# Moving the first query and key load and a 360-element load in a fused one-core kernel, and two small copies from ScalarE to GpSimd

## The chip, the cores and the metric

The kernel runs on one core of a Trainium2 chip. The metric is the time of one execution in microseconds of device time. Before the change it is 308.97 us, the median of three runs (307.27 to 309.54).

## What is computed

Three layers run one after the other on an input of 2 batches, 768 positions and 8 heads of 40 elements, in single precision. The first is a recurrent attention layer with exponential gates:

```python
m_new = np.maximum(f_gate[:, :, t] + m, i_gate[:, :, t])
f_stab = np.exp(f_gate[:, :, t] + m - m_new)
i_stab = np.exp(i_gate[:, :, t] - m_new)
C = f_stab * C + i_stab * outer(v_t, k_t)
n = f_stab * n + i_stab * k_t
y[:, :, t] = sigmoid(o_gate_t) * (C @ q_t) / max(|n . q_t|, 1)
```

The second multiplies half of `relu(x @ w_in)` by a normalised and position-mixed other half, and by `w_out`. The third mixes each position with the one before it and applies `w_k`, `w_v` and `w_r`.

## The kernel before, in words

**Blocks.** The recurrence is computed in chunks of 128 positions. There are 12 blocks (2 batches x 6 chunks), taken in the order of the list `SEQ`: chunk 0 of both batches, then chunk 1 of both, and so on. This text calls them block 0, block 1, block 2 and block 3 by their place in that order. Per block TensorE makes scores `sc` from queries and keys `qk` (line 463), a logarithmic decay `ld` (lines 471 to 475, or 495 from block 4 on), the inside part `av` (line 599), the state update `sp` from weighted keys `kw` (line 533), the part that comes from the state `cn` (`ip`, line 570), and at the end a transpose `tp` of the finished rows `x` (line 646). ScalarE takes the exponential of `ld` into `dt` (line 479), VectorE multiplies `dt` by `sc` (line 489). The transposed rows go into `xg` (a rounded part from ScalarE, line 660, and a rest from VectorE, line 235), and feed the products `up` and `vp` with `w_in`, which begin at about 35 us and keep TensorE filled from there on. All the later layers are matmuls of line 671.

**Who sets the order.** A planner in Python keeps an estimated clock for TensorE, VectorE, ScalarE and GpSimd and writes their instructions in the order that this clock gives; each engine then runs its list strictly in that order, and waits on semaphores for the others. Where the planner expects TensorE to be idle in the first blocks it writes dummy matmuls (`heat`, line 363, output `wp`). They are a fixed number of instructions, run whether or not TensorE would have had to wait.

**Loads.** Nearly all transfers are issued by the SyncE queue (SP), in the order of the code. Each takes one of eight semaphores in turn, so that a transfer is not issued before the one eight places ahead of it has landed. The first ones are the gates `fg` and `ig`, the identity `id_sb`, four output gates `og` (160 KB each), the queries and keys of block 0 in two halves of 160 KB (each 40 rows of 4 KB), then `kvq` of block 0, a third of `w_in`, the queries and keys of block 1, and so on. `bm_raw`, three columns of the block mask in 120 rows, is 360 separate elements of 4 bytes.

**The mask and the output gates.** ScalarE first takes the sigmoid of the four `og` tiles as they land (line 355), then copies the identity to `mask[:, 1]` (line 859), and only then begins with the exponentials. TensorE's third matmul of each first `ld` (line 475) reads that mask.

**The state.** For chunk 0 ScalarE copies `bm_raw` to `bm_sb` (line 546) and writes `cn` from `sp` with it (line 548). For later chunks `cn` is first multiplied by `dec` (line 543). `dec`, and the gate rows of all later chunks, come from a chain over all chunks at once, called G1 in the code: `f<-f,m`, `i<-i,m`, `f<-f,m`, a scan, and so on (lines 407 to 416) on VectorE, with two casts (`Lxc`, `Axc`) on ScalarE. Its end is `i<-i,f` (line 416), which TensorE transposes into `gpsc` (line 423). Two small transfers per row pair (`lt`, `rl`) then bring its results to where line 495 reads them.

**The repeated columns of x.** Each finished block `x` has 320 columns, and its columns 256 to 320 are copied to 320 to 384 (lines 627 and 628) before the transpose. For blocks 0 and 1 ScalarE makes this copy, for all others GpSimd.

**The weights.** The three thirds of `w_u` are split into two parts by a chain: two ScalarE operations (`wsq`, `wbits`, lines 274 and 278), two of VectorE (lines 284 and 288), a cast on ScalarE (line 297) and a subtraction on GpSimd (line 235).

Of the kernel before, what the change touches and what calls it, by code (L numbers as in the profile page):

```python
# [7 lines left out]
F32 = mybir.dt.float32  # L8
# [10 lines left out]
def tile_mlstm_gmlp_channelmix(  # L19
# [25 lines left out]
    SEQ = [6 * b + c for c in range(6) for b in range(2)]  # L45
    P = 128
    H, D = 8, 40
    DA = D + 1
# [3 lines left out]
    DM = H * D  # L52
# [6 lines left out]
    vec, act, pool, pe = nc.vector, nc.scalar, nc.gpsimd, nc.tensor  # L59
    sync = nc.sync  # L60
# [4 lines left out]
    at = tc.alloc_tile_pool(name="at", bufs=1, side="right")  # L65
# [59 lines left out]
    def use(e, cost, t=None):  # L125
        free[e] = max(free[e], clock[0] if t is None else t) + cost
        return free[e]
# [45 lines left out]
    def chain(key, *steps, ready=None):  # L173
        running.append(Chain(key, steps, clock[0] + 0.2 if ready is None else ready, 0.0))

    def finish(*keys, stall=True):
        for k in keys:
            while any(b[0] == k or b[0][0] == k for b in back):
                if not force_feed():
                    break  # L180
            for c in [c for c in running if c.has(k)]:
                while c in running and c.has(k):
                    advance(c.start(), skip=c)
                    if not c.open():
                        finish(split[0], stall=False)
                    if c in running and c.has(k):
                        issue(c)
        if stall:
            at_least(max([done.get(k, 0.0) for k in keys], default=0.0))
# [25 lines left out]
    def load(out, in_, kb, after=0.0):  # L215
        sync.dma_start(out=out, in_=in_)  # L216
        dma_free[0] = max(dma_free[0], after, clock[0] - 1.0) + max(0.5, kb / (360.0 if clock[0] > 20.0 else 230.0))
        return dma_free[0] + 1.8

    def page(name, dt=F32R, n=PG, keys=()):  # L220
        own("pg", 12, *keys)
        return base.tile([P, n if dt == I64 else PG], dt, tag="pg", name=name, bufs=12)[:, :n]
# [80 lines left out]
    def rows3(t, w):  # L303
        return t[:, :3 * w].rearrange("p (a b) -> p a b", a=3)
# [6 lines left out]
    fg = gp.tile([16, S], F32, name="fg")  # L311
    ig = gp.tile([16, S], F32, name="ig")
# [17 lines left out]
    def load_qk(i):  # L330
        b, c = divmod(i, NCH)
        t = at.tile([P, 2, 4, P], F32, tag="qk", name=f"qk{i}", bufs=2)
        for hh in range(2):
            e = load(t[64 * hh:64 * hh + D], qk[b, c, hh], 164)
        st["q", i], st["k", i] = t[:, 0], t[:, 1]
        st["at", i] = e

    def load_kv(i):
        b, c = divmod(i, NCH)
        n = H * D + H * DA + (3 * P if c > 0 else 0)  # L340
        t = at.tile([P, H * D + H * DA + 3 * P], F32, tag="kvq", name=f"kvq{i}", bufs=2)
        note(("kv", i), load(t[:, :n], kvq[b, c, :, :n], n * 0.5))
        st["kt", i] = t[:, :H * D].rearrange("p (h d) -> p h d", h=H)
        st["vt", i] = t[:, H * D:H * (D + DA)].rearrange("p (h d) -> p h d", h=H)
        if c > 0:
            st["qc", i] = t[:120, H * (D + DA):].rearrange("p (g t) -> p g t", g=3)

    def load_o(c):
        for b in range(B):
            o = st["o", b, c] = at.tile([P, DM], F32, tag="og", name=f"og{c}_{b}", bufs=9)  # L350
            st["ot"] = load(o, o_tok[b, c // 3, :, c % 3], 164)
# [15 lines left out]
    vec.memset(unit.bitcast(F32), 0.0)  # L367
    for t in first_.values():
        vec.memset(t.bitcast(F32), 0.0)
    for a in 'f i d o0 o1 q'.split():  # L370
        dict(f=lambda: sync.dma_start(out=fg, in_=f_gate), i=lambda: sync.dma_start(out=ig, in_=i_gate),
             d=lambda: sync.dma_start(out=id_sb, in_=ident), o=lambda: load_o(int(a[1])), q=lambda: load_qk(SEQ[0]))[a[0]]()

    pool.memset(ones, 1.0)
# [227 lines left out]
    def normalise(i):  # L602
        b, c = divmod(i, NCH)
        av, spare = st.pop(("av", i)), st.pop(("spare", i))
        osl = st["o", b, c].rearrange("p (h d) -> p h d", h=H)
        nn = st.pop(("nn", i)) if c > 0 else at.tile([P, H, DA], F32, tag="nn", name=f"nn{i}", bufs=2)
        dn = at.tile([P, H], F32, tag="dn", name=f"dn{i}", bufs=2)
        x = at.tile([P, 3 * P], F32, tag="x", name=f"x{i}", bufs=2)

        finish(*[("nn", i)] * (c > 0), stall=False)  # L610

        def clip():
            vec.tensor_scalar(out=spare, in0=nn[:, :, D], scalar1=1.0, scalar2=None, op0=ALU.max)
            pool.tensor_tensor(out=osl, in0=osl, in1=nn[:, :, :D], op=ALU.mult)
            return use("P", 0.82, free["V"])

        chain(("x", i),
              ("V", 0.41, lambda: vec.tensor_tensor(out=nn, in0=nn, in1=av, op=ALU.add)) if c > 0 else
              ("A", 0.4, lambda: act.copy(nn, av)),
              ("V", 0.08, clip),  # L620
              ("V", 0.15, lambda: vec.scalar_tensor_tensor(out=dn, in0=nn[:, :, D], in1=spare,
                                                           scalar=-1.0, op0=ALU.mult, op1=ALU.max), ("av", i)),
              ("V", 0.18, lambda: vec.reciprocal(out=dn, in_=dn)),
              ("V", 0.4, lambda: vec.tensor_tensor(out=x[:, :DM].rearrange("p (h d) -> p h d", h=H), in0=osl,
                                                   op=ALU.mult,
                                                   in1=dn.unsqueeze(2).to_broadcast([P, H, D]))),
              ("P", 0.2, lambda: pool.tensor_copy(x[:, DM:], x[:, 2 * P:DM])) if SEQ.index(i) >= 2 else
              ("A", 0.2, lambda: act.copy(x[:, DM:], x[:, 2 * P:DM])))
        st["x", i] = x

    xg = {}
# [139 lines left out]
    def w_in_load(nm, j, *qs):  # L771
        W.setdefault((nm, "raw"), [])
        for q in qs:
            raw = page(f"w_in{nm}{q}", I64, PG // 2, [f"w_{nm}{x}" for x in range(3)])[:, :512]
            W[nm, "raw"].append((q, raw, load(raw, w_in[j, q], 512)))
# [84 lines left out]
    free["A"] = 8.5  # L860
    free["P"] = 3.0
    hu = [rows3(page(f"w_u{q}"), 512) for q in range(2)]
    bm_raw = at.tile([120, 3], F32, name="bm_raw")
    m2 = gp.tile([96, 2, P], F32, name="m2")
    lpk = gp.tile([96, 6 * NCH], F32, name="lpk")
    clock[0] = 5.5
# [4 lines left out]
        for w in range(2):  # L871
            st["late"] = load(m2[:, w], mg[:, w:w + S], 48, 14.0)

    for a in 'k0 v0 q6 k6 v1 b v2 n'.split():
        dict(k=lambda: load_kv(SEQ[a != "k0"]), q=lambda: load_qk(SEQ[1]), n=lambda: load_qk(SEQ[2]),
             v=lambda: w_in_load("u", 0, int(a[1])), b=lambda: load(bm_raw, blockmask[:, 0:3 * DA:DA], 2))[a[0]]()
    w_in_split("u", hu)
# [42 lines left out]
    def position(p):  # L920
# [45 lines left out]
        def n1():  # L966
            intra(i, 1)
            normalise(i)
            if nn is not None:
                load_kv(nn)  # L970
            if p == 0:
                w_in_load("v", 1, 0)
                sync.dma_start(out=mu_sb, in_=mu)
            if p == 1:
                w_in_load("v", 1, 1)
                load_o(2)
                load_o(3)
            if p == 2:
                w_in_load("v", 1, 2)
                load_o(4)  # L980
            if p == 3:
                load_o(5)
            if n is not None:
                key_weights(n)
# [225 lines left out]
    for g in range(2 * B):  # L1210
# [17 lines left out]
        for j in range(3):  # L1228
            sl = slice(j * P, (j + 1) * P)
            prs = []  # L1230
            for f in range(8):
                k0, k1 = k2t[g, f][:, 0, sl], k2t[g, f][:, 1, sl]
# [126 lines left out]
```

## Time and profile before

| | us |
|---|---|
| median of three runs | 308.97 |
| the profiled execution, its own time | 308.54 |
| its span, first to last instruction | 305.5 |
| TensorE busy in the span | 294.4 |
| VectorE busy | 218.5 |
| ScalarE busy | 172.4 |
| GpSimd busy | 140.3 |

The profile shows one execution. A timeline row has the start, the duration (for a group of neighbours the length from the first's start to the last's end), the engine, the line, the operation, output and input, and the count; in square brackets stands how long the engine was idle just before, and what ended that. Single-precision matmuls are recorded as two passes each. Names stand without their numbers, so that `qk` is any block's; the place in time tells which.

### The profile page before, as it was taken

To read this page: it belongs to the slowest core of one execution; us is meant where nothing else is said; L and a number is where in the kernel's file an instruction comes from. 1 tells how busy PE (TensorE), PEld (TensorE's weight loads), DVE (VectorE), ACT (ScalarE), POOL (GpSimd) and SP (SyncE) were. 2 spreads that over 40 slices of the span, in tenths; PEclk is the share of its full clock that TensorE was granted. 3 is DMA by queue.
4 is the path that set the end of the run, shared out by engine and by line. 5 is a ranking of instruction groups with operands and counts; after the bars stand their busy time and mean duration, and the time that the engine had idled before them with its cause. 6 is when DMAs were issued, how large, how long until landed. Compare 5 with 4: busy or idle time off the path is not lost.

```text
span 305.5 us, 6000 instructions
## 1 busy us (share of the span) xinstructions
PE 294.4 (96%) x2233; PEld 273.3 (89%) x2233; DVE 218.5 (72%) x440; ACT 172.4 (56%) x383; POOL 140.3 (46%) x167
## 2 busy tenths in 40 slices
PE   8998898999889999999999999999999999999995
PEld 6776787787778887999999999999999999999995
DVE  7768696856697787746879989898856755745611
ACT  3764587676865555653254654686936845734610
POOL 5143324526679774733556637484426305303500
PEclk9999999999999999999999999999999999999999
DMA  6959665333223411554115212221010010000001
GB/s 154 291 165 288 195 226 171 137 116 114 56 69 98 138 46 50 174 157 165 43 45 172 81 41 86 89 86 44 3 43 21 2 43 24 0 35 32 1 21 43
DMA packets 13939, 28.77 MB, mean 94 GB/s; under 512 B 2407, under 2 KB 7783, under 8 KB 13911
## 3 DMA queue, kind: packets, MB, share of 16 engines
q1 hardware_dynamic: 13879, 28.33, 29.4%
q8 instruction: 17, 0.28, 0.4%
q0 software_dynamic: 32, 0.07, 0.2%
q14 instruction: 11, 0.09, 0.1%
HBM read 26.20 MB, written 1.97 MB: 92 GB/s over the span
## 4 chain that ended last, share of the span: by engine, by line
PE 71%; DVE 9%; ACT 6%; POOL 5%; DMA 4%; issue 2%; SPq 1%; POOLq 0%; DVEq 0%; ACTq 0%
PE spp L671 16%; PE kp L671 15%; PE vv L671 14%; PE wop L671 7%; PE up L671 5%; PE rp L671 5%; DMA bm_raw<-in_blockmask_dram 3%; PE vp L671 2%; DMA qk<-in_qk_dram 2%; POOL vn L235 2%; PE sc L463 1%; DVE sb L728 1%; DVE dt L508 1%; PE av L599 1%; SPq L216 1%
## 5 line engine op out<-in xcount | busy, mean ns | idle before, releaser
L1202 POOL TENSOR_TENSOR sq<-sq 128x384 f32<-128x384 f32 x32 | 29.9, 941 | 47.9 <-ACT sq L1201 47.8
L671 PE MATMUL spp<-wsp,vn 128*128 128x384 f32 x288 | 50.4, 334 | 0.0
L671 PEld LDWEIGHTS spp<-wsp,vn 128*128 128x128 f32 x288 | 49.9, 188 | 0.0
L671 PE MATMUL kp<-xk,wk 128*128 128x384 f32 x256 | 45.3, 334 | 0.0
L671 PEld LDWEIGHTS kp<-xk,wk 128*128 128x128 f32 x256 | 44.4, 188 | 0.0
L671 PE MATMUL vv<-wv,k 128*128 128x320 f32 x288 | 42.9, 309 | 0.0
L671 PEld LDWEIGHTS vv<-wv,k 128*128 128x128 f32 x288 | 42.4, 188 | 0.0
L235 DVE TENSOR_TENSOR k<-sq,k 128x384 fp32r<-128x384 f32 x32 | 26.2, 820 | 13.6 <-ACT k L1203 13.6
L671 PE MATMUL up<-xg,w_u 128*128 128x256 f32 x192 | 31.0, 295 | 0.0
L671 PE MATMUL vp<-w_v,xg 128*128 128x512 f32 x96 | 29.0, 417 | 1.9 <-ACT vr L740 0.9
L1099 POOL TENSOR_TENSOR vs<-vs,u 128x384 f32<-128x384 f32 x16 | 19.8, 1237 | 22.5 <-DVE vs L1098 21.1
L671 PEld LDWEIGHTS up<-xg,w_u 128*128 128x128 f32 x192 | 25.8, 190 | 1.0 <-DVE xg L235 0.2
L1201 ACT ACTIVATE sq<-kp 128x384 f32<-128x384 f32 x32 | 15.6, 490 | 16.8 <-PE kp L671 14.8
L284 DVE SCALAR_TENSOR_TENSOR wbits<-wsq,wbits 128x320 int32<-128x320 int32 (+1 forms) x27 | 20.9, 774 | 4.4 <-ACT wsq L274 3.5
L671 PE MATMUL wop<-gt,wo 128*128 128x384 f32 x128 | 22.8, 334 | 0.0
L671 PEld LDWEIGHTS wop<-gt,wo 128*128 128x128 f32 x128 | 22.2, 188 | 0.0
L671 PEld LDWEIGHTS vp<-w_v,xg 128*128 128x128 f32 x96 | 17.0, 189 | 5.7 <-ACT vr L740 1.4
L1242 DVE TENSOR_TENSOR ob<-rs,vv 128x320 f32<-128x320 f32 x12 | 5.8, 487 | 20.4 <-PE vv L671 19.3
L235 POOL TENSOR_TENSOR vn<-vr,vn 128x512 fp32r<-128x512 f32 x12 | 15.4, 1287 | 6.8 <-ACT vn L750 6.8
L1100 ACT CAST gt<-vs 128x384 fp32r<-128x384 f32 x16 | 8.2, 512 | 18.0 <-POOL vs L1099 18.0
L288 DVE SCALAR_TENSOR_TENSOR wsq<-wraw,wbits 128x320 int32<-128x320 int32 (+1 forms) x21 | 17.2, 821 | 0.3
L1141 DVE SCALAR_TENSOR_TENSOR tm<-x,mu_sb,tm 128x384 f32<-128x384 f32 x24 | 17.1, 748 | 0.0
(184 smaller groups left out, 571.4 us busy)
## 6 DMA issues: line engine op xcount, KB each, us to landing
kvq<-in_kvq_dram SPq DMA_DIRECT2D x10, 516.0 KB
qk<-in_qk_dram SPq DMA_DIRECT2D x24, 160.0 KB
wraw<-in_w_k_dram SPq DMA_DIRECT2D x6, 512.0 KB
wraw<-in_w_v_dram SPq DMA_DIRECT2D x8, 320.0 KB
wraw<-in_w_sp_dram SPq DMA_DIRECT2D x12, 192.0 KB
og<-in_o_tok_dram SPq DMA_DIRECT2D x12, 160.0 KB
out_dram<-ob SPq DMA_DIRECT2D x12, 160.0 KB
w_inu<-in_w_in_dram SPq DMA_DIRECT2D x3, 512.0 KB
```

What stands on the lines that cost most here:

```text
L216: sync.dma_start(out=out, in_=in_)
L235: eng.tensor_tensor(out=out, in0=a, in1=b.bitcast(F32), op=ALU.subtract)
L284: vec.scalar_tensor_tensor(out=t["bits"], in0=t["sq"].bitcast(I32), scalar=3, in1=t["bits"], op0=ALU.logical_shift_left, op1=ALU.bitwise_or)
L288: vec.scalar_tensor_tensor(out=t["sq"].bitcast(I32), in0=t["high"], scalar=SIGN, in1=t["bits"], op0=ALU.bitwise_and, op1=ALU.bitwise_or)
L463: pe.matmul(st["sc", i, x][:, h * P:(h + 1) * P], k_[64 * x:64 * x + D, h, :], q_[64 * x:64 * x + D, h, :], start=True, stop=True)
L671: pe.matmul(out[0], l, x, start=j == 0, stop=j == len(prs) - 1)
L1099: ("P", 1.29, lambda: pool.tensor_tensor(out=vs, in0=vs, in1=ut[b][:, d, sl], op=ALU.mult)),
L1100: ("A", 0.51, lambda: act.copy(gt[:, 0], vs)), ("V", 0.7, lambda: sub(vec, gt[:, 1], vs, gt[:, 0])))
L1141: return lambda: vec.scalar_tensor_tensor(out=t[:, c], in0=x[:, c, 1:], scalar=mu_sb[:, w, c:c + 1], in1=t[:, c], op0=ALU.mult, op1=ALU.add)
L1201: chain(("k2", g, f), ("A", 0.49, lambda: act.activation(out=sq, in_=ps, func=AF.Relu), ("kp", g, f)), ("P", 0.96, lambda: pool.tensor_ten ...
L1202: ("P", 0.96, lambda: pool.tensor_tensor(out=sq, in0=sq, in1=sq, op=ALU.mult)),
L1242: vec.tensor_tensor(out=ob, in0=rs, in1=ps, op=ALU.mult)
```

## The change

The list of the first loads, a letter per load, becomes `f i d q b o0 o1` where it was `f i d o0 o1 q`: the queries and keys of block 0 (`q`) go ahead of the four output gates (`o0`, `o1`), and `bm_raw` (`b`) is loaded there too, behind the identity and the queries. It is taken out of the later list, where it stood between the second and the third part of `w_in`. The copy of the repeated columns is made by GpSimd for blocks 0 and 1 too.

```diff
-    for a in 'f i d o0 o1 q'.split():
-        dict(f=lambda: sync.dma_start(out=fg, in_=f_gate), i=lambda: sync.dma_start(out=ig, in_=i_gate),
+    bm_raw = at.tile([120, 3], F32, name="bm_raw")
+    for a in 'f i d q b o0 o1'.split():
+        dict(b=lambda: load(bm_raw, blockmask[:, 0:3 * DA:DA], 2), f=lambda: sync.dma_start(out=fg, in_=f_gate), i=lambda: sync.dma_start(out=ig, in_=i_gate),
              d=lambda: sync.dma_start(out=id_sb, in_=ident), o=lambda: load_o(int(a[1])), q=lambda: load_qk(SEQ[0]))[a[0]]()
...
-              ("P", 0.2, lambda: pool.tensor_copy(x[:, DM:], x[:, 2 * P:DM])) if SEQ.index(i) >= 2 else
-              ("A", 0.2, lambda: act.copy(x[:, DM:], x[:, 2 * P:DM])))
+              ("P", 0.2, lambda: pool.tensor_copy(x[:, DM:], x[:, 2 * P:DM])))
...
-    bm_raw = at.tile([120, 3], F32, name="bm_raw")
...
-    for a in 'k0 v0 q6 k6 v1 b v2 n'.split():
+    for a in 'k0 v0 q6 k6 v1 v2 n'.split():
```

On the SP queue, the first loads before the change; a name in brackets is the semaphore that the instruction waits for:

```order
L372 DMA id_sb<-in_ident_dram 128x128
L216 DMA og_0_103<-in_o_tok_dram 128x320
L216 DMA og_1_105<-in_o_tok_dram 128x320
L216 DMA og_0_107<-in_o_tok_dram 128x320
L216 DMA og_1_109<-in_o_tok_dram 128x320
L216 DMA qk_111<-in_qk_dram 40x1024
L216 DMA qk_111<-in_qk_dram 40x1024 [waits DMAHW0_49]
L216 DMA kvq_153<-in_kvq_dram 128x648 [waits DMAHW1_49]
```

The same stretch after the change:

```order
L373 DMA id_sb<-in_ident_dram 128x128
L216 DMA qk_104<-in_qk_dram 40x1024 x2
L216 DMA bm_raw<-in_blockmask_dram 120x3x1
L216 DMA og_0_108<-in_o_tok_dram 128x320
L216 DMA og_1_110<-in_o_tok_dram 128x320
L216 DMA og_0_112<-in_o_tok_dram 128x320 [waits DMAHW0_49]
L216 DMA og_1_114<-in_o_tok_dram 128x320 [waits DMAHW1_49]
L216 DMA kvq_154<-in_kvq_dram 128x648 [waits DMAHW2_49]
```

The two halves of `qk` and `bm_raw` now stand ahead of all four `og`.

On ScalarE, from the first copy of `x` to the second (between about 20 and 33 us in the profile), before the change. The names are those of the paragraphs above; `w_u` is the cast of line 297:

```order
L628 COPY x_347<-x_347 128x64
L297 CAST w_u_148<-wsq 128x512
L660 CAST xg_412<-tp_413 128x3x128
...
L414 CAST Axc<-i_77 96x128
L628 COPY x_489<-x_489 128x64
L297 CAST w_u_148<-wsq 128x512
L479 ACTIVATE dt_0_539<-ld_0_532 128x512
L426 ACTIVATE egc<-gpsc 128x192
L910 ACTIVATE dec<-dps 120x36
L543 ACTIVATE cn_323<-cn_323,dec 120x123 x2
```

After the change, where line numbers differ by one or so:

```order
L660 CAST xg_407<-tp_408 128x3x128
L297 CAST w_u_150<-wsq 128x512
...
L415 CAST Axc<-i_77 96x128
L480 ACTIVATE dt_0_538<-ld_0_531 128x512
L427 ACTIVATE egc<-gpsc 128x192
L909 ACTIVATE dec<-dps 120x36
L297 CAST w_u_150<-wsq 128x512
L544 ACTIVATE cn_323<-cn_323,dec 120x123 x2
```

The two copies are gone, the first `xg` cast stands ahead of the first `w_u` cast, and the exponential `dt_0_538` of block 3 and `dec` stand ahead of the third `w_u` cast.

On VectorE one operation of the third part of `w_u`, `wbits<-wsq,wbits`, goes from ahead of the G1 chain to behind the second block's `x`. Before:

```order
L288 SCALAR_TENSOR_TENSOR wsq<-w_inu_162,wbits 128x512
L284 SCALAR_TENSOR_TENSOR wbits<-wsq,wbits 128x512
L407 TENSOR_TENSOR f_76<-f_76,m_151 96x128
L408 TENSOR_TENSOR i_77<-i_77,m_151 96x128
...
L624 TENSOR_TENSOR x_489<-og_1_105,dn_488 128x320
L288 SCALAR_TENSOR_TENSOR wsq<-w_inu_165,wbits 128x512
```

After:

```order
L288 SCALAR_TENSOR_TENSOR wsq<-w_inu_163,wbits 128x512
L408 TENSOR_TENSOR f_76<-f_76,m_152 96x128
L409 TENSOR_TENSOR i_77<-i_77,m_152 96x128
...
L625 TENSOR_TENSOR x_488<-og_1_110,dn_487 128x320
L284 SCALAR_TENSOR_TENSOR wbits<-wsq,wbits 128x512
L288 SCALAR_TENSOR_TENSOR wsq<-w_inu_165,wbits 128x512
```

The G1 chain now follows `wsq` of the second part directly. On TensorE the only difference of order is that the first transpose `tp` stands two dummy matmuls earlier; the number of matmuls is the same.

## Rows read from the trace of the kernel before

**Rows 1.** The page: span, busy time of each engine, granted TensorE clock in 40 slices.
```profile
span 305.5 us, 6000 instructions
PE 294.4 (96%) x2233; PEld 273.3 (89%) x2233; DVE 218.5 (72%) x440; ACT 172.4 (56%) x383; POOL 140.3 (46%) x167
PEclk9999999999999999999999999999999999999999
```
**Rows 2.** The chain that ended last, first 50 us: start, length, what.
```profile
4.08 4.69 DMA qk<-in_qk_dram
...
8.79 8.23 DMA bm_raw<-in_blockmask_dram
```
**Rows 3.** Timeline of TensorE, 0 to 40 us.
```profile
8.52 0.39 PE L475 MATMUL ld<-mask 128*128 128x512 bf16 x1
...
14.15 0.48 PE L463 MATMUL sc<-qk 40*128 40x128 f32 x2
14.91 1.13 PE L463 MATMUL sc<-qk 40*128 40x128 f32 x14 [0.28 <-DMA qk<-in_qk_dram]
...
18.80 2.02 PE L363 MATMUL wp<-id_sb 128*128 128x256 bf16 x12
...
27.38 0.48 PE L471 MATMUL ld<-unit,Axb 128*128 128x512 f32 x1 [0.59 <-DVE dt L489]
...
29.50 0.30 PE L423 MATMUL gpsc<-id_sb,i 96*128 96x96 f32 x1 [0.71 <-DVE i L416]
...
32.27 0.80 PE L533 MATMUL sp<-kvq,kw 128*120 128x123 f32 x6 [1.22 <-ACT dt L479]
...
39.06 0.50 PE L495 MATMUL ld<-rl,lt 128*128 128x512 f32 x1
```
**Rows 4.** Timeline of the SP queue, 0 to 26 us (issue times and lengths).
```profile
4.08 0.74 SPq L216 DMA_DIRECT2D qk<-in_qk_dram  x2
...
8.79 0.36 SPq L216 DMA_DIRECT2D bm_raw<-in_blockmask_dram  x1
10.01 0.33 SPq L216 DMA_DIRECT2D w_inu<-in_w_in_dram  x1
```
**Rows 5.** Timeline of ScalarE, 4 to 18 us.
```profile
7.81 0.47 ACT L355 ACTIVATE og<-og 128x320 f32<-128x320 f32 x1 [1.59 <-DMA og<-in_o_tok_dram]
8.19 0.28 ACT L859 CAST mask<-id_sb 128x128 bf16<-128x128 f32 x1
...
17.04 0.19 ACT L546 COPY bm_sb<-bm_raw 120x3 f32<-120x3 f32 x1 [1.84 <-DMA bm_raw<-in_blockmask_dram]
```
**Rows 6.** Timeline of ScalarE, 20 to 32 us.
```profile
20.52 0.62 ACT L297 CAST w_u<-wsq 128x512 fp32r<-128x512 f32 x1
21.19 0.48 ACT L660 CAST xg<-tp 128x384 fp32r<-128x384 f32 x1
...
24.16 0.59 ACT L479 ACTIVATE dt<-ld 128x512 f32<-128x512 f32 x1
...
30.41 0.24 ACT L628 COPY x<-x 128x64 f32<-128x64 f32 x1 [2.46 <-DVE x L624]
31.01 0.62 ACT L297 CAST w_u<-wsq 128x512 fp32r<-128x512 f32 x1 [0.36 <-DVE wsq L288]
31.54 0.59 ACT L479 ACTIVATE dt<-ld 128x512 f32<-128x512 f32 x1
```
**Rows 7.** Timeline of VectorE, 23 to 30 us.
```profile
24.39 1.36 DVE L407 TENSOR_TENSOR f<-f,m 96x128 f32<-96x128 f32 x1
...
26.64 0.69 DVE L489 TENSOR_TENSOR dt<-dt,sc 128x512 f32<-128x512 f32 x1
```
**Rows 8.** Timeline of GpSimd: the copy as it makes it for block 2.
```profile
39.12 0.29 POOL L627 COPY x<-x 128x64 f32<-128x64 f32 x1 [1.07 <-DVE x L624]
```
**Rows 9.** Stretches: busy PE, PEld, DVE, ACT, POOL; granted clock, DMA share, GB/s.
```profile
8.40:10.00 1.60, 1.60 (x13) 1.20 (x11) 1.44 (x6) 1.57 (x3) 0.00 (x0) 1.00 1.03 274
34.00:34.50 0.50, 0.50 (x6) 0.50 (x5) 0.24 (x2) 0.00 (x0) 0.00 (x0) 1.00 0.08 25
```

## The prediction

> **What bounds the kernel now.** I read the page first: TensorE is busy for 294.4 us of a span of 305.5 [rows 1]. From about 35 us on it is filled by matmuls whose number the change leaves alone. What can be won or lost is therefore TensorE's waiting in the first 35 us, and whatever moves TensorE there moves the end by the same amount, unless something later takes it back. The chain of waits, read next, goes through the landing of the first `qk` (4.08 to 8.77 us) and of `bm_raw` (8.79 to 17.02 us) [rows 2], the two transfers that the change brings forward. But the chain says only what ended last; whether TensorE stood still for it is in its own timeline. There five places tell [rows 3]:
> - `ld<-mask` at 8.52. The mask was cast on ScalarE from 8.19 to 8.47, behind the sigmoid of the fourth `og`, which began at 7.81, when that tile landed, after 1.59 us of idle time [rows 5]. So TensorE is already tied to the fourth `og`: landing, plus 0.71 us, is the start of this matmul.
> - The scores of block 1: two matmuls at 14.15, the other 14 at 14.91, ended by a `qk` landing. The 14 last 1.13 us, some 0.08 apart, so the third could have begun at about 14.3; it lost 0.6 us, more than the 0.28 of modelled idle time.
> - 0.59 us at 27.38 until VectorE's `dt`, 0.71 us at 29.50 until `i<-i,f`, the end of the G1 chain, and 1.22 us at 32.27 until ScalarE's `dt` of block 3.
>
> Neither the wait for `bm_raw` (1.84 us, ScalarE, at 17.04 [rows 5]) nor one for the first `qk` stands on TensorE: at 18.80 it has 12 dummy matmuls ahead of the transpose that the chain leads to [rows 3].
>
> **The loads: a loss.** The first `qk` moves ahead of four `og`, and is needed later than they are, since the scores stand behind `ld<-mask`. When does the fourth `og` land now? Lower bound: it moves only by what is issued ahead of it, 0.74 us for two `qk` and 0.36 for `bm_raw` [rows 4], with the gaps some 1.15 us, so at 8.95. Upper bound: transfers land in the order of issue, and the same bytes now end with the `og`. `bm_raw`'s issue at 8.79 and the next one's at 10.01 each waited for one half of the first `qk` (they stand eight places behind), so the whole set had landed by 10.0 [rows 4]. With 0.4 us for 360 small packets in front (an estimate: as much as `bm_raw`'s own issue; no row separates their cost, and nothing would be the lower end) that is 10.4. I take 9.8, 2.0 us later, nearer to the upper end, because the two halves landed 1.22 us apart: 160 KB in that time is 134 GB/s while all transfers together moved 274 GB/s [rows 9], so `qk` is held by some of the engines only, and an `og`, which needs them too, waits behind it.
>
> The Trainium skill, page DMA: Bandwidth & Descriptors, section on why a DMA increments its semaphore by 16, says that a transfer is spread over the largest number of engines up to 16 that divides its rows: 10 engines for 40 rows, 16 for 128. The half rate agrees with it. By that rule alone the `og` would land with the old end of `qk`, at 10.0, and the sum below would be 0.2 us higher.
>
> So `ld<-mask` starts 2.0 us late (1.15 to 2.6), at about 10.5. Queued behind it on TensorE are the rest of both `ld`, four dummy matmuls and the scores, and on ScalarE the table load and the exponentials; all move with it. The wait at the scores of block 1 gives back its 0.6 us, since TensorE now comes after that `qk` has landed. **Late by 2.0 - 0.6 = 1.4 us** (0.55 to 2.0) from there on; call it s.
>
> `bm_raw` early takes away ScalarE's 1.84 us of idle time, and what stood behind (`cn`, `nn`) then waits for TensorE's `sp` instead, which is s late. Gain on TensorE: none, since the transpose stands behind dummy matmuls, two fewer than before. If these did not cover it, it could gain up to 0.4 us, the 1.84 less `sp`'s own 1.4.
>
> **The copies: a gain.** GpSimd's copy costs 0.29 us [rows 8] where ScalarE's cost 0.24 [rows 6]. The first is covered by ten dummy matmuls (12 take 2.02 us [rows 3]). The second waits for `x`, which is there at 30.41 [rows 6] plus the 0.36 us found below, and is done at 31.1, before TensorE starts the `sp` that stands ahead of the second transpose. Without that cover the price is 0.05 us each. What counts is the order that it leaves behind on ScalarE and VectorE.
>
> First, the G1 chain. The transpose ends s - 0.3 late (two dummy matmuls of 2.02/12 us go behind it). ScalarE casts `xg` (0.48) at 20.9 + s and only then begins with `w_u`, at 21.36 + s where it was 20.52. From that cast to `dt` of block 2 (24.16) are 3.64 us of cast, GpSimd subtraction, two operations and a second cast, which keep their order; so `dt` runs from 25.0 + s to 25.6 + s. VectorE waits for it: it no longer has `wbits` ahead of the chain, and even if `f<-f,m` again takes 1.36 us [rows 7], it reaches its own `dt` before that. So VectorE's `dt` starts at 25.6 + s where it was 26.64 [rows 7], a change of s - 1.04 us, and `i<-i,f`, six operations on, follows it. With s = 1.4 TensorE's `gpsc` comes at 29.86 instead of 29.50. The 0.59 us are gone (`ld` of block 3 has its predecessor in time), and most of the 0.71: **gain 1.04 us**.
>
> Second, the 1.22 us. TensorE's `sp` of block 2 needs the bank that ScalarE's `dt` of block 3 (31.54) leaves. Before it ScalarE stood for 2.46 us, waiting for VectorE's `x` to copy its columns, then 0.36 us for the `w_u` cast [rows 6]. Both are now off its path: that `dt` follows the `Axc` cast directly, as soon as `ld` is there. TensorE starts that `ld` at 28.2 (27.38 - 0.59 + 1.4) and arrives at `sp` at 31.4 (32.27 + 0.36 - 1.22), 3.2 us later, while the `dt` itself takes 0.59. **Gain 1.22 us.** Late next is the third `w_u` cast, behind a VectorE operation more (some 0.7 us, as `dt` [rows 7]) and 0.36 us: at about 32 instead of 31.01. Its GpSimd half is needed only by the eighth `up` matmul, behind two `av`, a transpose and an `ld`.
>
> **The sum**, against the profiled execution's own 308.54 us (0.43 below the median of the runs): 308.54 + 2.0 - 0.6 - 1.04 - 1.22 = **307.7 us**. With the two bounds of the landing it is 306.8 and 308.3.
>
> **The rivals.**
> - *The `og` land hardly later than they are issued* (8.95), since engines serve several transfers at once: 308.54 + 1.15 - 0.6 - 2.26 = 306.8, and 306.4 if the `bm_raw` term's 0.4 came on top. Against it stands the order of landings.
> - *Slower: the rows of block 4 become the wait.* The last `rl` transfer is queued behind loads that wait for TensorE's `av` of block 1, so it lands s late, while TensorE would reach `ld<-rl,lt` at 38.2 instead of 39.06 [rows 3]. If they land past 39.06 the gains are lost and s stays: 308.54 + 1.4 = 309.9. It decides only if they landed within 1.4 us of use before; against it, transfers had all but stopped by 34.0 to 34.5 (25 GB/s [rows 9]).
> - *The change does not do what it says:* ScalarE's own row of work further on takes the gain back, and the loss with it: 308.5.
> - *The clock falls.* The granted clock is 1.00 (2.4 GHz) throughout [rows 1], also beside the wait of 1.22 us; a wait of 2.0 has no row. At 1.2 GHz the 5.6 us from the mask at 8.52 to the scores at 14.15 [rows 3] would double at most: 308.54 + 1.4 + 5.6 - 2.26 = 313.3. The Trainium skill, page TensorE: Matmul & The Clock Gate, Part 1, says that an idle stretch can halve the clock; no run here shows it for so short a one.
>
> **How the numbers follow.** Forecast 0.47, early landing 0.22, nothing 0.14, late rows 0.12, clock 0.05. A measurement of this kernel can tell about 1% (3.1 us) from no change. Only early landing, with its term and a low run, reaches past that downward (0.08), only the clock and a part of the late rows upward (0.06): same 0.86. The range runs from early landing with its 0.4, less some of the runs' own spread (305.9), to the late rows (309.9).
>
> **What would show it.** In the changed profile the fourth sigmoid should start near 9.8, `ld<-mask` near 10.5 after a wait of about 2 us, the scores of block 1 without a wait near 16.3, no wait of over 0.3 us at `sp` of block 2 near 31.4, and line 495 near 38.2. If the sigmoid starts before 9 the early landing holds; if 495 waits, the late rows. A wait at the first transpose for GpSimd's copy would make the cover wrong.

## The result and the profile after

The changed kernel takes 305.39 us (median of nine executions), the kernel before 308.46 beside it; the ratio is 0.9892, 95% interval 0.986 to 0.9924, so 1.1% faster. Three of the nine (311.0 to 312.5 us, mean granted clock 0.975 to 0.978) are left out of the ratio, as such slow executions are from the ratios below; the other six take 304.9 to 305.7 with spans of 303.1 to 303.7. The profiled execution took 305.08 us with a span of 303.1, 2.4 below the span of [rows 1]. The forecast was 307.7, the range 305.9 to 309.9: the median lies below it, and those three executions lie above it.

The page of the changed kernel, as in [rows 1]:
```profile
span 303.1 us, 5998 instructions
PE 293.2 (97%) x2233; PEld 272.7 (90%) x2233; DVE 218.3 (72%) x440; ACT 171.9 (57%) x381; POOL 141.1 (47%) x169
PEclk9999999999999999999999999999999999999999
```
TensorE runs the same 2233 matmuls, so what went is its waiting. The page shows only half of that as idle time (9.9 us against 11.1) and the other half as busy time (293.2 against 294.4): a busy matmul can hold a wait, as the scores of block 1 did in [rows 3], 0.28 us idle for 0.6 lost. The timeline is the better witness. TensorE's timeline, at the places of [rows 3] (start, length, line, what, and in brackets the idle time before it and what ended it):
```profile
9.48 0.39 PE L476 MATMUL ld<-mask 128*128 128x512 bf16 x1 [1.29 <-ACT mask L859]
...
15.11 1.16 PE L464 MATMUL sc<-qk 40*128 40x128 f32 x16
...
20.57 0.49 PE L646 MATMUL tp<-id_sb,x 128*128 128x128 f32 x3
...
26.95 0.48 PE L472 MATMUL ld<-unit,Axb 128*128 128x512 f32 x1
...
28.50 0.30 PE L424 MATMUL gpsc<-id_sb,i 96*128 96x96 f32 x1
...
29.89 0.73 PE L534 MATMUL sp<-kvq,kw 128*120 128x123 f32 x6
...
36.61 0.50 PE L496 MATMUL ld<-rl,lt 128*128 128x512 f32 x1
```
Read against [rows 3], the first matmul with the mask is 0.96 us late (9.48 against 8.52), the scores of block 1 run without a wait, `gpsc` is 1.00 early, `sp` of block 2 is 2.38 early and line 496 (495 before) is 2.45 early. No wait is left at 26.95, 28.50 and 29.89. The end keeps those 2.4 us.

ScalarE in the changed kernel, as in [rows 5] and [rows 6]:
```profile
8.35 0.88 ACT L355 ACTIVATE og<-og 128x320 f32<-128x320 f32 x2 [0.20 <-DMA og<-in_o_tok_dram]
9.14 0.28 ACT L859 CAST mask<-id_sb 128x128 bf16<-128x128 f32 x1
...
16.08 0.19 ACT L547 COPY bm_sb<-bm_raw 120x3 f32<-120x3 f32 x1
17.15 0.82 ACT L549 ACTIVATE cn<-sp,bm_sb 40x123 f32<-40x123 f32 x3 [0.88 <-PE sp L534]
...
28.09 0.60 ACT L480 ACTIVATE dt<-ld 128x512 f32<-128x512 f32 x1 [1.05 <-PE ld L476]
...
30.74 0.62 ACT L297 CAST w_u<-wsq 128x512 fp32r<-128x512 f32 x1 [1.37 <-DVE wsq L288]
```
The fourth sigmoid, second of the pair at 8.35, begins near 8.8 where it began at 7.81. `bm_sb` no longer waits, but `cn` behind it waits 0.88 us for TensorE. The `dt` of block 3 now stands ahead of the `w_u` cast and waits only for its own `ld`. VectorE and GpSimd, as in [rows 7] and [rows 8]:
```profile
25.75 0.69 DVE L490 TENSOR_TENSOR dt<-dt,sc 128x512 f32<-128x512 f32 x1 [0.71 <-ACT dt L480]
...
27.82 0.63 DVE L417 TENSOR_SCALAR i<-i,f 96x128 f32<-96x128 f32 x1
```
```profile
19.77 0.63 POOL L628 COPY x<-x 128x64 f32<-128x64 f32 x1 [0.59 <-DVE x L625]
...
29.44 0.63 POOL L628 COPY x<-x 128x64 f32<-128x64 f32 x1 [1.07 <-DVE x L625]
```
VectorE's `dt` is 0.89 us earlier and the end of the G1 chain, `i<-i,f`, 1.00. GpSimd's copies take 0.63 us each, twice the 0.29 of [rows 8].

### The profile page after: what moved, and what is told of

Read it like the earlier page. It is cut to its first block, busy times and chain, and to the rows that moved or that the text cites. A ratio compares the mean times of both kernels' runs of the same rounds, so it can differ in the third digit from the quotient of the medians.

```text
span 303.1 us, 5998 instructions
## 1 busy us (share of the span) xinstructions
PE 293.2 (97%) x2233; PEld 272.7 (90%) x2233; DVE 218.3 (72%) x440; ACT 171.9 (57%) x381; POOL 141.1 (47%) x169
## 4 chain that ended last, share of the span: by engine, by line
PE 76%; DVE 8%; ACT 6%; POOL 5%; issue 2%; DMA 1%; SPq 1%; POOLq 0%; DVEq 0%; ACTq 0%
PE spp L671 16%; PE kp L671 15%; PE vv L671 14%; PE wop L671 7%; PE up L671 5%; PE rp L671 5%; PE vp L671 2%; PE sc L464 2%; PE av L600 2%; POOL vn L235 2%; PE sp L534 1%; DMA og<-in_o_tok_dram 1%; DVE sb L728 1%; DVE dt L509 1%; SPq L216 1%
```

## The experiments

**The kernel before, again.** No edit.

> The kernel before, once more as a kernel of its own, to see the span of every run beside its time (so far only one run of it shows both: 308.54 us with a span of 305.5, 3.04 us around the span, while the changed kernel's runs have 1.7 to 2.0 us around it). Theory A (the change moves TensorE in the first 32 us and nothing else): the spans lie at 305.5 within 0.3 us and the times at 307.5 within 0.3 us. Rival B (the kernel before has a start that varies from run to run, since one of its early waits does): the spans themselves spread over 1 us or more, as its times do (307.03 to 309.54).

Measured: median 308.38 us, ratio 0.9987 (0.9957 to 1.0018), with spans of 305.4 to 308.0: rival B holds. Its profile is not that of [rows 1]: the span is 308.0 and the granted clock falls in the fifth of 40 slices. The PEclk row of the page, TensorE's timeline, and four stretches (busy PE, PEld, DVE, ACT, POOL; granted clock, DMA share, GB/s):
```profile
PEclk9999599999999999999999999999999999999999
```
```profile
26.97 0.48 PE L471 MATMUL ld<-unit,Axb 128*128 128x512 f32 x1 [0.61 <-DVE dt L489]
...
29.09 0.30 PE L423 MATMUL gpsc<-id_sb,i 96*128 96x96 f32 x1 [0.71 <-DVE i L416]
...
31.86 1.42 PE L533 MATMUL sp<-kvq,kw 128*120 128x123 f32 x6 [1.22 <-ACT dt L479]
...
41.48 0.49 PE L495 MATMUL ld<-rl,lt 128*128 128x512 f32 x1
```
```profile
29.00:32.00 3.00, 1.69 (x12) 1.35 (x13) 1.72 (x7) 1.64 (x5) 0.70 (x1) 0.87 0.89 306
32.00:35.00 3.00, 3.00 (x26) 2.42 (x27) 1.79 (x6) 0.97 (x4) 1.25 (x2) 0.50 0.35 109
35.00:38.00 3.00, 3.00 (x18) 2.47 (x18) 0.72 (x2) 0.89 (x2) 0.00 (x0) 0.50 0.12 45
38.00:41.00 3.00, 3.00 (x41) 2.82 (x39) 2.15 (x7) 0.94 (x4) 0.81 (x1) 0.99 0.39 88
```
The three waits are those of [rows 3], to 0.02 us. But in the last of them the granted clock falls from 1.00 (2.4 GHz) to 0.50 (1.2 GHz), and it stays there until about 38 us. From the start of `sp` to line 495 TensorE takes 9.62 us (41.48 - 31.86), against 6.79 in [rows 3] (39.06 - 32.27): the fall costs 2.8 us.

It is common. Of the 66 executions of the kernel before that stood beside the experiments, 25 have a mean granted clock of 0.997 or more and spans with a median of 305.2 us (time 307.0); 41 have 0.994 or less (the lowest 0.986) and a median span of 307.4 (time 309.4). The execution that I had read before predicting was one of the minority.

**The loads alone.**
```
-    for a in 'f i d o0 o1 q'.split():
+    for a in 'f i d q b o0 o1'.split():
...
-    for a in 'k0 v0 q6 k6 v1 b v2 n'.split():
+    for a in 'k0 v0 q6 k6 v1 v2 n'.split():
```


> Only the moved loads; ScalarE still copies the columns of blocks 0 and 1, and every compute engine has the order of the kernel before. Theory A: the fourth og lands 0.9 to 1.0 us later, the mask's ld starts at 9.5, the scores of block 1 give back 0.6 to 0.7 us, the waits of 0.6, 0.7 and 1.2 us at 27 to 32 us all stay; the time is 0.2 to 0.3 us over the kernel before (308.7). Rival B (bm_raw off ScalarE's path is worth something by itself): 0.5 to 0.9 us under the kernel before (307.7).

Measured: ratio 0.9985 (0.9949 to 1.002). Two rows of its TensorE timeline:
```profile
9.78 0.39 PE L476 MATMUL ld<-mask 128*128 128x512 bf16 x1 [1.98 <-ACT mask L860]
...
32.51 0.73 PE L534 MATMUL sp<-kvq,kw 128*120 128x123 f32 x2 [1.22 <-ACT dt L480]
```
The loads win nothing. The mask comes late and the 1.22 us are still there. Of the twelve executions four kept a clock of 1.00, five have 0.987 to 0.994, as in the kernel before, and three have 0.967 to 0.973 and take 314.9 to 316.5 us, which no execution of the kernel before does.

**The copies alone.**
```
-              ("P", 0.2, lambda: pool.tensor_copy(x[:, DM:], x[:, 2 * P:DM])) if SEQ.index(i) >= 2 else
-              ("A", 0.2, lambda: act.copy(x[:, DM:], x[:, 2 * P:DM])))
+              ("P", 0.2, lambda: pool.tensor_copy(x[:, DM:], x[:, 2 * P:DM])))
```


> Only the two copies to GpSimd; the loads stand as before, and every compute engine has the order of the changed kernel. Theory A: mask's ld at 8.5 and bm_raw landing at 17.0 as before; gpsc 1.04 us earlier and sp of block 2 2.3 us earlier than before; time 306.2 or less, so within 0.3 us of the changed kernel or up to 0.3 below. Rival B: the gain is shared, 306.5 to 307, a good part over the changed kernel's 305.4.

Measured: 304.58 us, ratio 0.9858 (0.9823 to 0.9894); `sp` of block 2 starts at 29.08 without a wait, and the clock is 0.998 or more in all six executions. The copies, with the order that they leave behind, carry the whole gain. To size the loads I ran this kernel once more beside the changed one in one job.

> The changed kernel itself, beside the one with the copies alone in the same job, to size what the early loads cost. Theory: ld<-mask again at 9.3 to 9.8, 0.7 to 1.5 us later than with the loads of before, of which the wait for block 1's queries gives back up to 0.7; median 305.1 to 305.7. Rival (the loads cost nothing): the same median as the copies alone, within 0.3.

> Only the copies on GpSimd, loads as before, in the same job as the changed kernel. Theory: 304.4 to 304.9, 0.4 to 1.0 us below the changed kernel, ld<-mask at 8.2 to 9.0. Rival: within 0.3 of it.

Measured: the changed kernel 305.27 (median of six; ratio 0.9891, 0.9847 to 0.9935), the copies alone 304.99 (0.9884, 0.9844 to 0.9923). My theory of 0.4 to 1.0 us falls and the rival holds, but for executions that keep their clock only: over both jobs the copies alone have a median span of 303.15 us (12 executions), the changed kernel 303.4 (the 10 of its 15 with 0.998 or more). The mask is 0.8 us or more later with the early loads, and the scores of block 1 give a part back: `sp` behind these starts at 15.03 and 15.85 in the two profiles of the copies alone, at 16.20 in the changed kernel's.

The other two of the six executions take 311.2 and 311.4 us at clocks of 0.978 and 0.976. With the three of the result that makes 5 of the changed kernel's 15, about 6 us longer; of the 33 executions with block 0's copy on GpSimd and the loads as before (here, above and below) none has a clock under 0.998. So the early loads are not free: they leave the typical execution where it was within 0.3 us, and a third of the executions lose 6 us.

**Which copy.** First block 0's copy alone goes to GpSimd, as below; then block 1's alone, with `!= 0` in the same place. From block 2 on GpSimd copies as before.
```
-              ("P", 0.2, lambda: pool.tensor_copy(x[:, DM:], x[:, 2 * P:DM])) if SEQ.index(i) >= 2 else
+              ("P", 0.2, lambda: pool.tensor_copy(x[:, DM:], x[:, 2 * P:DM])) if SEQ.index(i) != 1 else
```


> The kernel before, with GpSimd copying x's repeated columns of block 0 (and, as before, from block 2 on); block 1's copy stays on ScalarE, the loads stay as before. The planner then puts exp of block 3 ahead of the cast of w_u on ScalarE, and the transposition of block 0 ahead of two dummies on TensorE. Theory: this one copy carries nearly all of the gain, since it changes the order in which ScalarE reaches dt of block 3: sp of block 2 without a wait of over 0.5 us, clock at 0.997 or above in nearly all executions, 304.5 to 305.3. Rival (both copies are needed): sp waits 0.5 us or more, 306.5 to 308.5.

> The kernel before, with GpSimd copying x's repeated columns of block 1 alone; block 0's copy stays on ScalarE, loads as before. TensorE's and VectorE's order is unchanged, on ScalarE one copy is missing. Theory (the gain is the order, not the ScalarE time of a copy): sp of block 2 still waits, by 0.3 us less at most (about 0.9), spans as before or up to 0.3 below, the clock still falls in many executions, ratio 0.996 to 1.000. Rival (the 0.3 us of a copy on ScalarE is what counts): wait gone, ratio 0.985 to 0.992.

Measured: block 0's copy 305.17 us (ratio 0.9912, 0.9882 to 0.9941), block 1's 308.59 (1.0012, 0.9978 to 1.0046). ScalarE, with block 0's copy moved and then with block 1's:
```profile
29.03 0.24 ACT L628 COPY x<-x 128x64 f32<-128x64 f32 x1 [2.37 <-DVE x L624]
29.18 0.59 ACT L479 ACTIVATE dt<-ld 128x512 f32<-128x512 f32 x1
...
30.36 0.62 ACT L297 CAST w_u<-wsq 128x512 fp32r<-128x512 f32 x1 [0.27 <-DVE wsq L288]
```
```profile
31.11 0.62 ACT L297 CAST w_u<-wsq 128x512 fp32r<-128x512 f32 x1 [3.06 <-DVE wsq L288]
31.63 0.59 ACT L479 ACTIVATE dt<-ld 128x512 f32<-128x512 f32 x1
```
Taking block 1's copy off ScalarE leaves it idle for 3.06 us instead of 2.46 and 0.36 [rows 6], waiting for the next thing in its row, the `w_u` cast; `dt` of block 3 still stands behind that cast, and TensorE still waits 1.22 us. Moving block 0's copy leaves a copy in front of `dt`, with its wait, but makes the planner put `dt` ahead of the cast: the 1.22 us shrink to 0.24 and all 12 executions have a clock of 0.998 or more. So ScalarE's time for the second copy is worth nothing, and my expectation that its wait would shrink by up to 0.3 us was wrong too; what counts is the order. The pair differs in more of it than one cast: with block 0's copy moved, `xg` also stands ahead of `w_u` and VectorE's `wbits` behind the G1 chain, as in the changed kernel, and `gpsc` waits 0.16 us instead of 0.71. That the 1.22 us hang on the cast is read from the lines above; the two orders were not tried apart.

**Are the waits what costs the clock?** The kernel before, with dummy matmuls in two waits: six between the two transposes of `gpsc`, eleven ahead of `sp` of block 2. The planner does not count their time.
```
+    def spin(n):
+        wp = bank(psm, "mm", "wp")
+        for _ in range(n):
+            pe.matmul(wp[:, :256], id_sb.bitcast(BF16)[:, :P], id_sb.bitcast(BF16), start=True, stop=True)
...
+            if nm == "c" and w == 0:
+                spin(6)
...
+        if (best["slot"], best["p"]) == (2, 2):
+            spin(11)
```


> The kernel before, with dummy matmuls (256 columns each, as its own) put into two of TensorE's waits: six between the two transpositions of gpsc (wait of 0.71 us) and eleven ahead of sp of block 2 (wait of 1.22 us). Loads, copies and the order of everything else as before, and the planner's clock not moved. Theory (these waits make the granted clock fall in many executions, and each fall costs 2 to 3 us): the clock stays at 0.997 or above in nearly every execution, spans 305 to 306, median 307.0 to 307.5, ratio 0.993 to 0.996, and no execution at 309 or above except by what lies around the span. Rival (the clock falls for another reason, so the mixture of 307 and 309 stays): ratio 0.998 to 1.002. Second rival (the dummies delay the work behind them): ratio above 1.002.

Measured: 307.04 us, ratio 0.9968 (0.9939 to 0.9997). TensorE's timeline:
```profile
27.83 0.82 PE L369 MATMUL wp<-id_sb 128*128 128x256 bf16 x6
...
30.10 1.36 PE L369 MATMUL wp<-id_sb 128*128 128x256 bf16 x11
31.48 0.80 PE L540 MATMUL sp<-kvq,kw 128*120 128x123 f32 x6
...
38.27 0.50 PE L502 MATMUL ld<-rl,lt 128*128 128x512 f32 x1
```
`sp` still starts only when ScalarE lets it, and line 502 (495 before) follows after 6.79 us, as in [rows 3]. But 10 of the 12 executions have a clock of 0.999 or 1.00, against 8 of 32 of the kernel before in that job (15 with 0.997 or more); the other two have 0.994, with spans of 306.7 and 307.0. Useless work in the waits wins back most of what the falls cost, 1.4 us of the median, though the ratio's interval ends just below 1. Why two executions still fall (the wait ahead of `ld` of block 3 was left as it was) was not tried.

**The late gates.** The prediction's largest term was the fourth `og`. First `q` alone ahead of the gates (the first added line), then `b` (`bm_raw`) alone (the second, and taken out of the later list), the copies as before.
```
-    for a in 'f i d o0 o1 q'.split():
+    for a in 'f i d q o0 o1'.split():
+    for a in 'f i d b o0 o1 q'.split():
```


> The kernel before with the first queries and keys loaded ahead of the four output gates; bm_raw and the copies as before. The question is the term that the prediction set at 2.0 us. Issue alone (what is issued ahead, 0.74 us and a gap, is what the gates lose): the fourth sigmoid at 8.4 to 8.8, ld<-mask at 9.1 to 9.5. The prediction's picture (the gates end where the whole set ended before): fourth sigmoid at 9.4 or later, ld<-mask after 10.1.

> The kernel before with bm_raw loaded ahead of the four output gates; the queries and the copies as before. Issue alone: the gates lose 0.36 us and a gap, the fourth sigmoid at 8.0 to 8.4, ld<-mask at 8.7 to 9.1. If its 360 small packets hold the gates up: fourth sigmoid later than 8.7. Scores of block 1 still wait for their queries, by 0 to 0.6 us.

ScalarE and TensorE with `q` alone, then with `b` alone (one execution each):
```profile
8.15 1.56 ACT L355 ACTIVATE og<-og 128x320 f32<-128x320 f32 x3 [1.13 <-DMA og<-in_o_tok_dram]
9.61 0.28 ACT L859 CAST mask<-id_sb 128x128 bf16<-128x128 f32 x1
...
9.95 0.39 PE L475 MATMUL ld<-mask 128*128 128x512 bf16 x1 [1.37 <-ACT mask L859]
```
```profile
7.57 0.47 ACT L355 ACTIVATE og<-og 128x320 f32<-128x320 f32 x1 [0.16 <-DMA og<-in_o_tok_dram]
7.94 0.28 ACT L860 CAST mask<-id_sb 128x128 bf16<-128x128 f32 x1
...
8.39 0.39 PE L476 MATMUL ld<-mask 128*128 128x512 bf16 x1
```
`bm_raw`'s 360 packets cost nothing that shows: 8.39, earlier than I had expected (8.7 to 9.1). `q` alone gives 9.95, between my two expectations (9.1 to 9.5, or after 10.1). Taken over profiles, with the loads as before this matmul starts at 8.22 to 8.96 (seven profiles, mean 8.52); with `q` ahead, at 9.48, 9.70, 9.78 and 9.95 (mean 9.73). So the queries cost the gates 1.2 us, with a scatter of some 0.4 us either way that a single pair of traces does not show.

**The mask first.** ScalarE casts the mask ahead of the sigmoids, in the changed kernel, and then with the copies alone.
```
+    act.copy(mask[:, 1], id_sb)
     open_gate(0)
     open_gate(1)
-    act.copy(mask[:, 1], id_sb)
```


> The changed kernel with ScalarE's cast of the mask ahead of the four sigmoids instead of behind them, so that TensorE no longer waits for the fourth og. Theory A (that wait is what the loads cost): the mask's ld starts at about 8.1 without a wait, the scores of block 1 then wait for their qk (landed between 14.2 and 15.0), and everything behind is 0.2 to 0.9 us earlier: 304.8. Rival B (the exponentials, behind the table load and the sigmoids, hold the same stretch anyway): 305.4, no change.

> GpSimd copies both blocks, the loads stay in the order of before, and ScalarE casts the mask ahead of the four sigmoids. Theory (the early loads only delay the mask's cast, and the mask's way to TensorE is what the start waits for): as the changed kernel with the mask first, 304.15, or a little less, 303.6 to 304.3. Rival (with the loads as before the scores of block 1 wait for their queries as long as the mask saves, so early queries are worth something once the mask is out of the way): 304.4 to 305.

Measured: with the early loads 304.15 us (0.9837, 0.9802 to 0.9871), without them 304.94 (0.9913, 0.988 to 0.9946), in the rival's range and not the theory's. The first, on TensorE:
```profile
8.09 0.39 PE L476 MATMUL ld<-mask 128*128 128x512 bf16 x1
...
13.71 1.61 PE L464 MATMUL sc<-qk 40*128 40x128 f32 x16
```
The wait at the mask is gone, and all five executions have spans of 302.0 to 302.6, below every one of the changed kernel's in the two jobs; the scores of block 1 now wait for their queries inside the 1.61 us (1.16 without). It has the lowest median of all that I ran, with one line moved on top of the change; the copies alone had 304.58 in the same job, with spans of 302.0 to 303.9, so the two are not clearly apart. None of its five executions lost its clock, which is too few to set against 5 of 15. That it beats the one without the early loads because of these is not shown: the scores of block 1 take 1.60 us there too, and the two ran in different jobs.

## Why the prediction was wrong, step by step

Two terms of the sum failed, each by about 1 us: the base that it starts from, and the 2.0 us for the late `og`.

**The base of the sum.** I set the sum against the profiled 308.54 us, which is a span of 305.5 and 3.04 us around it. The six executions after that kept their clock have 1.7 to 2.0 around the span, the profiled one 1.98; so have 57 of the 66 of the kernel before. Of the 2.6 us between forecast (307.68) and profiled execution (305.08), 1.06 are this and 1.04 the next term. Nothing in the change acts there; I should have made the sum in spans. The text did say how 308.54 stands to the median, and took their closeness for agreement. It was a coincidence: a high clock with much around the span, beside a median of three executions whose clock had probably fallen (their clocks are not known).

**The loads: right mechanism, wrong size.** TensorE does wait at the mask for the fourth `og`, 0.7 us behind its landing. But the term of 2.0 us measured 0.96, below its lower bound of 1.15 (issue alone); over several profiles 1.2, about that bound. The failed step is "the same bytes now end with the `og`". It kept the end of the set at 10.0 and added to it; the changed kernel has the fourth `og` by 8.8. Two issues of its SP queue show when the queries had landed, since they stand eight places behind the two halves:
```profile
5.73 0.43 SPq L216 DMA_DIRECT2D w_inu<-in_w_in_dram  x1
6.26 0.88 SPq L216 DMA_DIRECT2D qk<-in_qk_dram  x2
```
The second half was in by 6.26, at most 4.1 us after the first one's issue at 2.18; before it took 5.9 (4.08 to 10.01 [rows 4]). So the end at 10.0 belonged to queries that came behind four `og`, and did not pass on to `og` that come behind queries. The rule that stood beside this step, from the Trainium skill (page DMA: Bandwidth & Descriptors, section on why a DMA increments its semaphore by 16), may hold for which engines carry a transfer, though no row names them; that the `og` end where the queries ended, at 10.0, is not what the trace shows (8.8). Why the set ends earlier in the new order stays open. So the rival "the `og` land hardly later than they are issued" is what happened. On the span its sum, -1.71, gives 303.8, against 303.1 measured; with 1.7 to 2.0 us around the span that is 305.5 to 305.8, where the base of 308.54 made it 306.8.

**The queries of block 1: right, with some luck.** They gave back 0.73 (0.96 at the mask, 0.23 at `sp`), 0.6 forecast. Over profiles it is less: `sp` starts at 15.63 on average in the seven with the loads as before, and at 16.46 in the three at a full clock with `q` ahead, 0.8 later, so 0.4 of the 1.2 us came back. In two of the seven the scores of block 1 took 1.16 us, with no wait to give back. `bm_raw`: right, no gain on TensorE; ScalarE waits for `sp` instead.

**The copies: right, and a little small.** With s = 0.23 instead of 1.4, the G1 step says s - 1.04, so -0.81 at `gpsc`; measured -1.00. Behind it the 1.22 us went and 0.16 more (1.38). The pair of single copies shows what the prediction named, the order left behind on ScalarE. The copies cost twice their estimate, 0.63 us; the ten dummy matmuls hid the first, and no wait shows behind the second.

**Line 495: right.** It does not wait at 36.61, so the late rows of block 4 were no danger, nor was the gain taken back further on.

In this pair of profiles the four terms come to +0.96 - 0.73 - 1.23 - 1.38 = -2.4 us on the span, where I had -0.86.

**What the forecast left out: the clock before.** The median moved by 3.1 us, more than those 2.4. I had one profile of the kernel before, with a granted clock of 1.00 throughout, and argued from it that the clock stands beside a wait of 1.22 us. In 41 of 66 executions it does not. All 38 executions of the variants above with both copies, or block 0's, on GpSimd have 0.998 or more, and 10 of the 15 of the changed kernel itself (the other five are the next point); kernels that keep the three waits have the mixture (before, loads alone, block 1's copy alone). Filling two of the waits moved most executions to the high clock, so these waits cause most of the falls. Compared at the high clock alone, the change is worth 307.0 - 305.2 = 1.8 us; executions whose clock had fallen gain about 4.2 (309.4 - 305.2).

**The clock rival stood at the other wait.** I gave it 0.05 at the new mask wait, at 313.3 us. In an execution of the changed kernel with a span of 309.4 the granted clock did fall there, behind a wait of 1.40 us, and is 0.50 from 12 to 24 us:
```profile
9.70 0.39 PE L476 MATMUL ld<-mask 128*128 128x512 bf16 x1 [1.40 <-ACT mask L859]
```
```profile
8.00:10.00 2.00, 0.60 (x5) 0.44 (x5) 1.87 (x8) 1.79 (x5) 0.00 (x0) 1.00 0.99 329
10.00:12.00 2.00, 2.00 (x13) 1.29 (x13) 0.53 (x3) 1.99 (x3) 0.00 (x0) 0.68 1.02 309
12.00:16.00 4.00, 4.00 (x25) 3.56 (x26) 2.03 (x4) 0.24 (x2) 1.49 (x3) 0.50 0.93 303
16.00:20.00 4.00, 4.00 (x33) 3.32 (x33) 1.30 (x1) 2.48 (x6) 0.54 (x2) 0.50 0.50 139
20.00:24.00 4.00, 4.00 (x36) 3.55 (x33) 1.89 (x3) 1.25 (x4) 0.00 (x0) 0.50 0.37 95
```
Five of its 15 executions have such spans (309.3 to 309.6); only this one has a trace. The price that I put on the fall, 5.6 us, is near the 6 us between this span and the others, but I took it as coming in all executions or in none. The length of the wait alone does not decide: with block 0's copy alone moved, the profile has 1.34 us at the same place, and none of those 12 executions lost its clock.

## What to carry to other kernels

Read several executions of the kernel before: if their spans fall into two groups by granted clock, a wait of TensorE of only a microsecond may cost three, and removing it, or filling it with dummy matmuls, pays more than its length. Count the executions whose clock falls after the change too: here a median hides a third of them. Make the sum in spans, and take what lies around the span from all executions, not from the profiled one. When an operation changes engine, look first at what it leaves in front of the instruction that TensorE waits for: here a copy's 0.24 us were worth nothing and the order left behind over 1 us.

## What the chip showed that was not expected

The same program kept its clock in 25 executions and lost it in 41. Two more have a trace, and both show the same waits (0.6, 0.7 and 1.2 us within 5 us, between matmuls that all ran at a granted clock of 1.00): one stayed at 1.00 throughout, in the other the clock was halved for some 7 us. The Trainium skill, page TensorE: Matmul & The Clock Gate, Part 1, says that an idle stretch can halve the clock; the runs agree, and show that it can turn on waits this short, in some executions and not in others. GpSimd's small copy took 0.23 to 0.56 us at its ten places in the kernel before, and 0.63 at its two new places in the changed one; the 0.29 that the forecast used was one of the ten.
